# In the last batch's attention, ScalarE takes five of six drawn key blocks and the neighbours' V rows from VectorE; three of the first expert tiles' row gathers move to the end of the attention

## The chip, the cores and the metric

The kernel runs on one core of a Trainium2 chip. The metric is device time in microseconds (us). A profiled execution has, beside its time, a span: the time from its first to its last instruction. Engines are called as the profile calls them: PE is the matrix engine (TensorE), PEld its loading of stationary operands, DVE is VectorE, ACT is ScalarE, POOL is GpSimd, and SP is the engine that here only issues transfers.

## What is computed

Two stages, in 32-bit floats. First, block-sparse attention over 4 batches, 8 heads, 768 positions and head dimension 64, in blocks of 32. Then a mixture of experts over the resulting 3072 rows of 512 values: each row goes to its best of 8 experts.

```python
# attention: a query block sees its neighbours, the first and last block, and three drawn blocks
mask = np.abs(blk_i - blk_j) <= 1
mask = mask | (blk_i == 0) | (blk_j == 0) | (blk_i == n_blocks - 1) | (blk_j == n_blocks - 1)
for qb in range(n_blocks):
    for kb in sampled_blocks[qb]:
        mask[qb * 32:(qb + 1) * 32, kb * 32:(kb + 1) * 32] = True
attn = softmax(where(mask, q @ k.T / 8, -1e9)) @ v
x = attn.transpose(0, 2, 1, 3).reshape(3072, 512)
# experts
expert_idx = argmax(x @ w_gate); gate_w = softmax(x @ w_gate)[row, expert_idx]
out[row] = gate_w * (relu(x[row] @ w1[expert_idx]) @ w2[expert_idx])
```

## The kernel before

**Attention in steps.** A batch has 24 query blocks. They are worked off in six groups (numbered g; the order is 5, 0, 1, 2, 3, 4), a group of four blocks as two tiles of 64 queries; group 5 has one such tile, and the first and last block, which see every key. Each group takes two steps, one for each half of the heads, so there are 12 steps per batch and 48 in all, numbered i from 0. Batch 3, the last, has steps 36 to 47. Step i does the following, and each engine executes its share in program order, since the order of the attention is written out by hand:

- copies for step i + 2: `place_middle` (DVE, the neighbouring keys into `xk`, L539 and L540), `place_keys` (the six drawn key blocks of one query tile into `kr`, L555: three on ACT, then three on DVE; each block is a copy of 128 partitions by 4 x 32 values, and its column comes from a register that the engine loads from `from_k`, L550);
- the scores of step i on PE (`s`, L339 and L344), the exponentials on ACT (`ea`, L349), and the masks on DVE (L355), two each;
- the products with V of step i - 1 on PE (`attend`, L373), chunk by chunk: chunk 0 is neighbours' rows, chunks 1 and 2 hold gathered rows;
- every second step, PE turns a finished block of rows (`turn_out`, `xr`, L464), ACT copies it (`xo`, L466) and PE makes the gate's logits (L482);
- the division on DVE (`divide`: `sums` L442, `r` L444, `xb` L448), and in odd steps SP's transfer of `xb` to `x_rows` in DRAM (L454);
- in odd steps `place_values` for the next group but one step: neighbours' V rows into `around`, on ACT (L532) and DVE (L533).

**V's gathered rows.** `fetch_values(b, g, ti, ch)` (L515) makes POOL issue an indirect transfer of 128 rows, or 64, of 2080 bytes from `v_rows` into `around`. Four are issued per group, each behind `not_before` (L527), a one-element copy on POOL that makes the queue wait for something that DVE writes: `sums`, `xk`, `kr`'s last block, or a masked `ea`. The last of a group's four, (ti, ch) = (1, 1), is issued at the head of the group's first step and read by PE one step later.

**The routing, inside batch 3.** The first three batches' rows are finished by then. `early` does their sorting in steps 38 to 44, almost all on DVE: ranks, counts (`cnA`, L771), the expert numbers `xeA` (L792), slots, one-hots (L960), and the row lists `gA` (L995). From step 40 on, SP fetches the first two experts' weights in 16 parts of 512 KB (L1081, L1085), two per step. SP takes its work in order: parts stand behind the `xb` transfers of L454.

**The experts.** `gather(i)` (L1041) makes POOL gather the 128 rows of expert tile i from `x_rows` into `xg`, 2080 bytes each; `turn_x(i)` turns them on PE (L1110), with an ACT copy (L1111); `layer1` and `layer2` (L1121, L1135) follow. `turn_x(0)` stands after the scores of step 47, `turn_x(1)` inside `layer1(0)`, `turn_x(2)` inside `layer1(1)`. The gathers 0, 1 and 2 are issued at the ends of steps 44, 45 and 46; gather 3 at the start of the expert loop.

Of the kernel before, what the change touches and what calls it, by code (L numbers as in the profile page):

```python
# [17 lines left out]
def kernel(  # L18
# [11 lines left out]
    nc = tc.nc  # L30
    P = 128
    B, H, S, D = q.shape
    BLK = 32
    NB = S // BLK
    NR = sampled_blocks.shape[1]
# [76 lines left out]
    def held(flat):  # L112
        a, c = NPR * S, 2 * NPR * S
        return (
            flat[:, :a].rearrange("p (r s) -> p r s", r=NPR), flat[:, a:c].rearrange("p (r s) -> p r s", r=NPR),
            flat[:, c : c + NCH * VR].rearrange("p (c w) -> p c w", c=NCH),
        )

    sets = [held(other[:]), held(room[:])]
    sets = [sets[(b + B - 1) % 2] for b in range(B)]  # L120
# [5 lines left out]
    around = mpool.tile([P, 2, 5, VR], F32, name="around")  # L126
# [167 lines left out]
    def tiles_of(g):  # L294
        return (2 * g, 2 * g + 1) if g < GL else (2 * g,)

    def parity(b, g):
        return (b * NG + order.index(g)) % 2
# [19 lines left out]
    def plan_all(b, pr):  # L318
        kT = sets[b][0][:, pr, :]
        return [(j, at_cols(kT, c * P + j * D, D), all_queries(b, pr), c * D, D) for c in range(NCH) for j in range(2)], []  # L320
# [117 lines left out]
    def divide(b, g, half):  # L438
        bank, _ = banks_of.pop((b, g, half))
        op = bank[:, : 4 * (D + 4)].rearrange("p (a w) -> p a w", a=4)  # L440
        mine = sums[:, b * NG + g, 4 * half : 4 * half + 4]
        nc.vector.tensor_scalar_add(mine, op[:, :, D], 1e-9)  # L442
        r = small.tile([P, 4], F32, name="r", bufs=2)
        nc.vector.reciprocal(r[:], mine)  # L444
        if half == 0:
            xbs[(b, g)] = work.tile([P, DM], F32, name="xb")
        xb = xbs[(b, g)]
        nc.vector.tensor_tensor(  # L448
            xb[:, half * 4 * D : (half + 1) * 4 * D].rearrange("p (a d) -> p a d", a=4), op[:, :, :D],
            r[:].unsqueeze(2).to_broadcast([P, 4, D]), op=ALU.mult,  # L450
        )
        if half == 1:
            for p, n, row in pieces(g):
                nc.sync.dma_start(x_d[b * S + row : b * S + row + n, :DM], xb[p : p + n, :])  # L454

    def pieces(g):
        if g < GL:
            return [(0, P, BLK + P * g)]
        return [(0, D, BLK + P * g), (D, BLK, 0), (D + BLK, BLK, S - BLK)]
# [65 lines left out]
    def not_before(at):  # L525

        nc.gpsimd.tensor_copy(paced[:], at)  # L527

    def place_values(b, g):

        par, n = parity(b, g), len(tiles_of(g))
        nc.scalar.copy(around[:D, par, 1 : 1 + n, :], sets[b][2][:D, g : g + n, :])  # L532
        nc.vector.tensor_copy(around[D:, par, 0, :], sets[b][2][D:, g, :])  # L533

    def place_middle(b, g):
        to, kT = xk[:, parity(b, g)], sets[b][0]
# [5 lines left out]
    def place_keys(b, g, ti, prs=slice(0, NPR), on_vector=NR):  # L542

        t = tiles_of(g)[ti]
        par = parity(b, g)
        cut = 2 * NR - on_vector
        for nm, a, z in (("Activation", 0, cut), ("DVE", cut, 2 * NR)):
            if a == z:
                continue
            _, at = nc.values_load_multi_w_load_instructions(  # L550
                from_k[0:1, NR + 2 * NR * t + a : NR + 2 * NR * t + z], engines=(getattr(mybir.EngineType, nm),),
                min_val=0, max_val=S - BLK, skip_runtime_bounds_check_because="clamped on the chip to the blocks that there are",
            )
            for i, v_ in zip(range(a, z), at):
                (nc.scalar.copy if nm == "Activation" else nc.vector.tensor_copy)(  # L555
                    kr[:, par, ti, prs, i * BLK : (i + 1) * BLK], sets[b][0][:, prs, bass.ds(v_, BLK)],
                )
# [478 lines left out]
    def of(name, i, p):  # L1036
        return rt[name + "A"][:p, i : i + 1] if i < KA else rt[name + "B"][:p, i - KA : i - KA + 1]

    def gather(i):
        xg = st[i]["xg"] = keep_xg[i % 4]  # L1040
        nc.gpsimd.indirect_dma_start(  # L1041
            out=xg[:], out_offset=None, in_=x_d[: N - S, :] if i < KA else x_d[:, :], in_offset=bass.IndirectOffsetOnAxis(ap=of("g", i, P), axis=0),
        )
# [250 lines left out]
    def fill_next(b, n):  # L1294
        fill_stage(b, n // 2, n % 2, n // 2 % 2)

    steps = [(b, g, half) for b in range(B) for g in order for half in range(2)]
    for i, (b, g, half) in enumerate(steps):
        here = i % (2 * NG)
        prs = (2 * half, 2 * half + 1)  # L1300
        nxt = steps[i + 2] if i + 2 < len(steps) else None

        if nxt is not None:
            b_, g_, half_ = nxt
            if half_ == 0:
                place_middle(b_, g_)
        if half == 0 and i > 0 and len(tiles_of(g)) > 1:
            if nxt is not None:
                not_before(xk[0:1, parity(*nxt[:2]), 0, D : D + 1])
            fetch_values(b, g, 1, 1)  # L1310
        if nxt is not None and half_ < len(tiles_of(g_)):
            place_keys(b_, g_, half_)
        two = half == 1 and i + 1 < len(steps) and len(tiles_of(steps[i + 1][1])) > 1
        if two:
            b_, g_, _ = steps[i + 1]
            not_before(kr[0:1, parity(b_, g_), 1, 0, NKR - 1 : NKR])
            fetch_values(b_, g_, 1, 0)

        if g == GL:
            plans = [plan_all(b, pr) for pr in prs if b > 0] + [plan_two(b, prs)]  # L1320
            *e_alls, e = scores(*plans)
            masked_two(e)
            mine = [(b, g, pr, e_alls[pr % 2] if b > 0 else None, e) for pr in prs]
        else:
            found = scores(*[plan(b, g, pr) for pr in prs])
            for e in found:
                masked(e, g)
            mine = [(b, g, pr, None, e) for pr, e in zip(prs, found)]
        if b == B - 1:
            early(here)  # L1330
        if half == 1 and i + 1 < len(steps):
            not_before(mine[1][4][0:1, 0, 0:1])
            fetch_values(*steps[i + 1][:2], 0, 1)

        copy_turned = None
        if b + 1 < B:
            if b == 0 and here < 2:
                fill_next(1, 2 * here)
                fill_next(1, 2 * here + 1)
            if 2 <= here < 10:  # L1340
                copy_turned = turn(b + 1, (here - 2) // 2, here % 2, None, (here - 2) // 2 % 2)
                if here < 6:
                    fill_next(b + 1, here + 2)
        if b + 2 < B and here >= 8:
            fill_next(b + 2, here - 8)

        out_of = steps[i - 3][:2] if i >= 3 and half == 1 else None
        if copy_turned:
            copy_turned()
        if i > 0 and before[0][1] != GL:  # L1350
            attend(before, (lambda: turn_out(*out_of)) if out_of else None)
        elif i > 0:
            for n, (b_, g_, pr, e_all, e) in enumerate(before):
                attend_last(b_, pr, e_all, e)
                if n == 0 and out_of:
                    turn_out(*out_of)
        if "gates" in rt:
            gate_weights()
        if out_of:
            logits(*out_of)  # L1360
            if out_of[1] == order[-1]:
                gate(out_of[0])
        if i > 0:
            divide(*steps[i - 1])
        if half == 0 and nxt is not None:
            if i >= 2:
                fetch_ends(*nxt[:2])
                b_, g_, half_ = steps[i - 1]
                not_before(sums[0:1, b_ * NG + g_, 4 * half_ : 4 * half_ + 1])
            fetch_values(*nxt[:2], 0, 0)  # L1370
        if half == 1 and nxt is not None:
            place_values(*nxt[:2])
        if b + 1 < B:
            load_v(b + 1, V_AT[b > 0].get(here, ()))
            if 7 <= here < 10:
                keep_v(b + 1, (2 * here - 14, 2 * here - 13))
        if 3 <= i < 11:
            route_consts(i - 3)
        if i == 11:
            route_tokens()  # L1380
        if b == B - 1 and 8 <= here < 11:
            gather(here - 8)
        before = mine
    turn_x(0)
    attend(before)
    divide(*steps[-1])
    attn_by_hand.close()
    lend(lent, ps_h=2, ps_m=2, ps_z=2)
    layer1(0, lambda: turn_out_late(*steps[-1][:2]), lambda: turn_x(1))
# [5 lines left out]
    for i in range(NS):  # L1395
# [4 lines left out]
        here = AT_S.index(i) if i in AT_S else None  # L1400
# [160 lines left out]
```

## Time and profile before

| what | us |
|---|---|
| median of 3 runs | 654.19 |
| the three runs | 651.63, 654.19, 657.99 |
| the profiled execution, time | 664.23 |
| the profiled execution, span | 662.5 |
| batch 3's stage of expert weights, 246.2 to 299.6 | 53.4 |
| experts after it, 299.6 to the end | 362.9 |

The profiled execution is 10.0 us above the median of the three runs. Its busy times are PE 628.4 us (95% of the span), DVE 305.1 (46%), ACT 223.7 (34%), POOL 182.8 (28%). These are averages over stages with different limits: between 240 and 250 us DVE is busy for 9.04 us of 10, and after 299.6 us for a third of the time. The profile gives all positions in us from the span's start, and a line such as L533 is line 533 of the kernel before.

### The profile page before, as it was taken

The numbers are of one execution on the slowest core, as the hardware profiler recorded it, in microseconds if no ns is written. First come the engines' busy times: TensorE is split into PE (matmuls) and PEld (weight loads), VectorE is DVE, ScalarE is ACT, GpSimd is POOL, SyncE is SP. The second block draws the span as 40 slices with busy tenths as digits, with TensorE's granted clock in tenths as the row PEclk, the third lists the DMA queues.
The fourth block names the chain that finished last, engine by engine and source line by source line (L and its number), as shares of the span: only waits on it lengthen the run. The fifth ranks groups of instructions, "written<-read, shape, count | busy, mean of one in ns | idle before, by whom it ended". The sixth has DMA issues, their size and how long they took to land. (4 is left out here: it accounts for less than half of the span.)

```text
span 662.5 us, 21377 instructions
## 1 busy us (share of the span) xinstructions
PE 628.4 (95%) x8952; PEld 524.3 (79%) x8952; DVE 305.1 (46%) x978; ACT 223.7 (34%) x430; POOL 182.8 (28%) x288
## 2 busy tenths in 40 slices
PE   7999999999999998789999999999999999999995
PEld 7888889998999887679776677797769678767962
DVE  6456665774677498632750368200182023702200
ACT  5456756675676554422111011121111111111110
POOL 2146744552354244710111122001300203020210
PEclk7769999999999996969999999999999999999998
DMA  9579966996787237954788999959996699989950
GB/s 266 168 189 231 250 181 157 217 264 171 172 199 218 81 98 267 308 189 165 263 315 303 352 348 347 342 206 361 400 398 245 209 405 395 343 286 391 396 205 19
DMA packets 124857, 170.93 MB, mean 258 GB/s; under 512 B 71028, under 2 KB 71029, under 8 KB 124726
## 3 DMA queue, kind: packets, MB, share of 16 engines
q1 hardware_dynamic: 114688, 137.61, 63.4%
q0 software_dynamic: 10000, 31.59, 14.7%
q8 instruction: 80, 1.31, 0.8%
q14 instruction: 51, 0.42, 0.2%
q10 hardware_dynamic: 38, 0.00, 0.0%
HBM read 150.11 MB, written 19.33 MB: 256 GB/s over the span
## 5 line engine op out<-in xcount | busy, mean ns | idle before, releaser
L1121 PEld LDWEIGHTS hp<-around,room 128*128 128x128 f32 x1216 | 138.4, 192 | 8.3 <-issue 5.6
L1121 PE MATMUL hp<-around,room 128*128 128x128 f32 x1216 | 141.3, 276 | 2.0 <-ACT kr L1128 1.7
L1102 DVE STREAM_TRANSPOSE around<-xg 32x128 f32<-32x128 f32 x208 | 62.9, 302 | 126.1 <-PE hp L1121 95.9
L349 ACT ACTIVATE ea<-s 128x768 f32<-128x768 f32 x104 | 81.4, 811 | 104.7 <-PE s L344 70.8
L1135 PE MATMUL zp<-room,kr 128*128 128x512 f32 x256 | 112.7, 594 | 0.0
L515 POOL DMA_INDIRECT around<-v_rows,rows_of x88 | 95.1, 1081 | 62.4 <-issue 23.7
L373 PE MATMUL op<-around,ea 128*64 128x65 f32 x2112 | 92.0, 232 | 6.2 <-DMA around<-v_rows,rows_of 3.4
L373 PEld LDWEIGHTS op<-around,ea 128*64 128x64 f32 x2112 | 79.9, 143 | 14.9 <-issue 6.3
L1135 PEld LDWEIGHTS zp<-room,kr 128*128 128x128 f32 x256 | 47.5, 190 | 54.6 <-issue 54.6
L355 DVE TENSOR_TENSOR ea<-ea,mask 128x768 f32<-128x768 f32 x80 | 74.4, 957 | 20.6 <-ACT ea L349 14.7
L1128 ACT ACTIVATE kr<-hp 128x512 f32<-128x512 f32 x36 | 21.4, 598 | 119.1 <-PE hp L1121 104.9
L1150 POOL DMA_INDIRECT out_dram<-kr,sB x14 | 14.1, 1006 | 164.6 <-ACT kr L1140 106.1
L1140 ACT ACTIVATE kr<-zp,xg 128x512 f32<-128x512 f32 x16 | 11.0, 690 | 100.3 <-PE zp L1135 100.3
L1228 DVE STREAM_TRANSPOSE ea<-ea 32x128 f32<-32x128 f32 x84 | 21.7, 285 | 32.6 <-DMA ea<-x_rows,gB 31.9
L1150 POOL DMA_INDIRECT out_dram<-kr,sA x5 | 5.1, 1020 | 89.8 <-ACT kr L1140 89.8
L344 PE MATMUL s<-other,kr 64*128 64x64 f32 x352 | 29.4, 273 | 0.5 <-issue 0.2
L339 PE MATMUL s<-room 64*64 64x64 f32 x736 | 27.2, 249 | 2.2 <-issue 1.9
L344 PE MATMUL s<-room,kr 64*128 64x64 f32 x352 | 28.5, 267 | 0.7 <-issue 0.5
L344 PEld LDWEIGHTS s<-other,kr 64*128 64x128 f32 x352 | 27.4, 201 | 1.0 <-issue 0.9
L344 PEld LDWEIGHTS s<-room,kr 64*128 64x128 f32 x352 | 26.3, 194 | 1.3 <-issue 1.3
L339 PE MATMUL s<-other 64*64 64x64 f32 x736 | 25.0, 231 | 1.9 <-issue 1.4
L339 PEld LDWEIGHTS s<-room 64*64 64x64 f32 x736 | 22.0, 158 | 4.8 <-issue 3.4
(342 smaller groups left out, 870.7 us busy)
## 6 DMA issues: line engine op xcount, KB each, us to landing
room<-in_moe_w_dram SPq DMA_DIRECT2D x46, 2048.0 KB
room<-in_moe_w_dram SPq DMA_DIRECT2D x16, 512.0 KB
x_rows<-xb SPq DMA_DIRECT2D x20, 256.0 KB
room<-in_k_dram SPq DMA_DIRECT2D x24, 192.0 KB
room<-in_q_dram SPq DMA_DIRECT2D x24, 192.0 KB
v_rows<-room SPq DMA_DIRECT2D x12, 260.0 KB
v_rows<-other SPq DMA_DIRECT2D x12, 260.0 KB
room<-in_v_dram SPq DMA_DIRECT2D x16, 192.0 KB
```

Of the source, the lines that this page charges most:

```text
L339: nc.tensor.matmul(s[j * D : (j + 1) * D, hh, a : a + n], lhsT=keys(r), rhs=queries(r), start=True, stop=True)
L344: nc.tensor.matmul(s[:, hh, a : a + n], lhsT=keys(r), rhs=queries(r), start=True, stop=True)
L349: nc.scalar.activation(e, s[:, :, : 6 * D], AF.Exp, scale=scale)
L355: nc.vector.tensor_tensor(e, e, m[:, None, :].to_broadcast([P, 2, 6 * D]), op=ALU.mult)
L373: nc.tensor.matmul(op[ti * D : (ti + 1) * D, pr % 2, hh, : D + 1], lhsT=e, rhs=values[:, (2 * pr + hh) * VW : (2 * pr + hh + 1) * VW], sta ...
L515: nc.gpsimd.indirect_dma_start(out=around[p0:, par, 1 + ti + 2 * ch, :], out_offset=None, in_=v_d[b][:, :], in_offset=bass.IndirectOffsetO ...
L1102: nc.vector.transpose(xT[d, :, t], xg[t, :DM].rearrange("p (c q) -> p c q", c=DB)[:, :, d])
L1121: nc.tensor.matmul(hp[:, m, :], lhsT=st[i]["w1"][:, c, fb * P : (fb + 1) * P], rhs=st[i]["xT"][:, c, :], start=(c == 0), stop=(c == DB - 1),)
L1128: nc.scalar.activation(hT[:, g * (FB // 2) : (g + 1) * (FB // 2), :], hp[:], AF.Relu)
L1135: nc.tensor.matmul(zp[:], lhsT=st[i]["hT"][:, fb, :], rhs=st[i]["w2"][:, fb, :], start=(fb == 0), stop=(fb == FB - 1),)
L1150: ins = nc.gpsimd.indirect_dma_start(out=to[:, :], out_offset=bass.IndirectOffsetOnAxis(ap=at, axis=0), in_=rows, in_offset=None, bounds_c ...
L1228: nc.vector.transpose(xT_u[d, :, j * P + tq * 32 : j * P + (tq + 1) * 32], xg_u[t, j, :DM].rearrange("p (c q) -> p c q", c=DB)[:, :, d],)
```

## The change

For the last batch only (`b == B - 1`), `place_keys` is called with one block on VectorE in place of three, so ScalarE copies five of six; and `place_values` has its second copy on ScalarE too. The gathers of the first three expert tiles are issued later: gather 0 at the end of step 46 (it was 44); gather 1 at the end of step 47 behind a wait of POOL for step 47's masked `ea` (it was 45, without a wait); gather 2 after the last division (it was 46). Gather 3, which follows in the program, is thus also behind that wait. PE's order is the same in both kernels.

```diff
@@ place_values @@
         nc.scalar.copy(around[:D, par, 1 : 1 + n, :], sets[b][2][:D, g : g + n, :])
-        nc.vector.tensor_copy(around[D:, par, 0, :], sets[b][2][D:, g, :])
+        (nc.scalar.copy if b == B - 1 else nc.vector.tensor_copy)(around[D:, par, 0, :], sets[b][2][D:, g, :])
@@ the loop over steps @@
         if nxt is not None and half_ < len(tiles_of(g_)):
-            place_keys(b_, g_, half_)
+            place_keys(b_, g_, half_, on_vector=1 if b_ == B - 1 else NR)
...
-        if b == B - 1 and 8 <= here < 11:
-            gather(here - 8)
+        if i == len(steps) - 2:
+            gather(0)
+        if i == len(steps) - 1:
+            not_before(mine[1][4][0:1, 0, 0:1])
+            gather(1)
         before = mine
     turn_x(0)
     attend(before)
     divide(*steps[-1])
+    gather(2)
     attn_by_hand.close()
```

## The prediction

> **What bounds the kernel now.** I first read the page's rows of 40 slices (16.6 us each: busy tenths, PE's granted clock, DMA share):
>
> ```profile
> PE   7999999999999998789999999999999999999995
> DVE  6456665774677498632750368200182023702200
> PEclk7769999999999996969999999999999999999998
> DMA  9579966996787237954788999959996699989950
> ```
>
> PE is full nearly everywhere, but in slices 16 to 18 (249 to 299 us, batch 3 and its weight transfers) it and its clock sag. So I read windows of 10 us there (columns: busy us with counts for PE, PEld, DVE, ACT, POOL; clock; DMA share; GB/s):
>
> ```profile
> 240.00:250.00 10.00, 9.02 (x228) 7.90 (x228) 9.04 (x34) 5.75 (x12) 5.78 (x7) 1.00 0.58 154
> 250.00:260.00 10.00, 7.86 (x126) 7.30 (x128) 7.56 (x26) 3.81 (x8) 5.55 (x8) 0.61 0.93 324
> 260.00:270.00 10.00, 9.72 (x234) 9.08 (x230) 9.16 (x26) 5.74 (x12) 5.18 (x6) 0.87 0.62 211
> 270.00:280.00 10.00, 7.62 (x158) 6.26 (x156) 5.70 (x19) 2.61 (x7) 6.85 (x10) 0.98 0.97 322
> 280.00:290.00 10.00, 6.54 (x83) 5.74 (x84) 2.17 (x6) 2.46 (x4) 3.05 (x4) 0.50 0.77 267
> ```
>
> There are two holes, at 250 and at 276 to 286, with the clock at 0.5 after each. The timeline of PE names what ended each stop (in brackets: idle before, releaser):
>
> ```profile
> 251.07 0.44 PE L464 MATMUL xr<-ident,xb 128*128 128x128 f32 x2 [1.33 <-DVE xb L448]
> ...
> 253.30 0.92 PE L373 MATMUL op<-around,ea 128*64 128x65 f32 x12 [1.06 <-DMA around<-v_rows,rows_of]
> ...
> 277.38 0.39 PE L373 MATMUL op<-around,ea 128*64 128x65 f32 x5 [0.77 <-DMA around<-v_rows,rows_of]
> 278.10 0.29 PE L373 MATMUL op<-around,ea 128*64 128x65 f32 x2 [0.33 <-issue]
> ```
>
> **Hole 1** is DVE's lateness (1.33 us), then a V gather's (1.06), then about 10 us at half clock. Scores ended at 248.28 in step 41 and 258.94 in step 42: 10.66 us, where steps 44 and 45 took 4.9 to 5.0. The hole costs 5.7 us: 2.4 of waits, 3.3 of clock. **Hole 2** is another thing. From 276.2 to 285.6 PE issues one to six matmuls, pauses, and starts again every 0.72 us, mostly with "issue" as releaser: no engine and no buffer holds it. Scores ended at 274.07 in step 45 and 289.4 in step 46: 15.3 us, 10.3 too many. After 299.6 us PE is busy 350.5 of 355.4 us (to 655), at full clock; nothing of the change reaches there unless a row gather is late.
>
> [...] clock 0.50 follows both holes. [...] The page's queue q8 has 80 packets in 1.31 MB, so blocks of that size; hole 2 looks like one that came late, which no run here has shown yet. [...] in 248 to 250 us SP's queue moved 0.57 MB of weights and POOL's queue nothing, with a V gather issued at 247.53.
>
> **The change part by part.**
>
> *DVE loses.* Batch 3 has 11 query tiles and 6 groups: 22 copies of key blocks and 6 of V rows leave it. The timeline has three blocks from 246.65 and the next work at 247.06, so 0.14 each; L533 from 246.00 to 246.44, 0.44. In all 22 x 0.14 + 6 x 0.44 = 5.7 us. Only what lies ahead of a wait counts:
>
> ```profile
> 246.00 0.43 DVE L533 COPY around<-other 64x520 f32<-64x520 f32 x1
> 246.44 0.29 DVE L540 COPY xk<-other 128x256 f32<-128x256 f32 x1
> 246.65 0.49 DVE L555 COPY kr<-other 128x128 f32 x3
> ...
> 250.59 0.42 DVE L448 TENSOR_TENSOR xb<-op,r 128x256 f32<-128x256 f32 x1
> ```
>
> From 240.4 to this `xb` DVE has no gap: it is the bound. Taken out on that run: in step 38, 0.44 + 0.28, of which 0.42 count (the second mask waits for the exponential that ends at 234.71); 0.28 in step 39; 0.44 + 0.28 in step 40: 1.42 us. `xb` ends at 249.6 in place of 251.02. PE also loses its wait of 0.54 for `cnA` at 242.2 and wants `xb` at 249.2, so about 0.4 remains of the two waits: at the transposes PE is 1.4 us ahead.
>
> *What is late next.* PE then wants the (1, 1) gather at 250.8 (before: 252.24, had at 253.30). Its issue follows `xk`, 1.14 us earlier. But the first two weight parts went out at 246.25, before it, and they follow `xeA`, which moves only 0.42 + 0.28 = 0.7 us; the gather's bytes came after them. So it lands 0.7 to 1.14 earlier, and I take 0.7: PE restarts at 252.6. Of 1.4 us, 0.7 goes into a longer wait for V. PE still idles some 2 us together[...], so the 3.3 us stay.
>
> *The same in step 45.* DVE runs without a gap from 264.32 to 273.6; 0.28 + 0.44 is taken out ahead of `xk` (270.15 on POOL), so the gather of 270.87 goes 0.7 earlier, against a wait of 0.77: gain 0 to 0.7, taken 0.5, as weights crowd it too.
>
> *ACT gains.* Two more blocks per tile at 0.20 (three span 0.70, the first 0.30): 0.40; in odd steps also a 64x520 copy, 0.59 by L532 of that shape (216.66 to 217.25). In all 22 x 0.20 + 6 x 0.59 = 7.9 us on an engine that is busy 5.75 of 10. Ahead of an exponential it has 2.57 us of idle time where both come (step 40), 0.99 used. Tightest is step 41:
>
> ```profile
> 246.51 0.70 ACT L555 COPY kr<-other 128x128 f32 x3
> 247.79 1.51 ACT L349 ACTIVATE ea<-s 128x768 f32<-128x768 f32 x2 [0.58 <-PE s L344]
> ```
>
> 0.58 of slack against 0.40, and PE comes up to 0.5 sooner: the exponential may be 0.3 late, hidden since its products come a step later. Queued behind the new copies are only exponentials and `xo`; `kr` is wanted two steps on. Cost 0, at most 0.3 in each of 5 such steps.
>
> *Waits and register loads.* The V copies' wait for the old `around` to be read is the wait that L532 has already passed on ACT. POOL's wait on `kr` reads block 5, which stays with DVE. SP's order changes in one thing: three loads of expert numbers slide behind four weight parts, where SP anyway waits for `xb`. Cost 0.
>
> *The row gathers.*
>
> ```profile
> 275.08 1.27 POOL L1041 DMA_INDIRECT xg<-x_rows,gA  x1 [0.30 <-issue]
> 276.35 0.18 POOL L527 COPY paced<-kr 1x1 f32<-1x1 f32 x1
> ...
> 280.51 0.95 POOL L515 DMA_INDIRECT around<-v_rows,rows_of  x1 [0.30 <-issue]
> ```
>
> Gathers 0 and 1 leave V's way on POOL: 1.27 + 1.25 us, so V's last gather is issued near 278. Gathers 1 to 3 leave the crowded stretch up to 287 us: 3 x 128 x 2080 B = 0.8 MB, 2.0 us at the 390 GB/s seen there. In this profile PE wants that V only at 295, long after it lands; with hole 2 absent it would want it near 287, and it would land near 286 (issued by 281.5, plus the 4.4 us that the gather of 247.53 took from its issue's end at 248.9 to PE's start). Gain 0 to 1.0, taken 0. POOL now waits for step 47's mask (296.94) ahead of gathers 1, 2, 3 and nothing else: gather 1 is issued by 298.4, landed by 302.8 at 4.4, wanted by `turn_x(1)` at 303.71; the two others follow 1.25 us apart, wanted at 312.06 and 326.64. Gather 0, issued near 280, is wanted after 287. Cost 0; if gather 1 takes 2 us longer, 1.1.
>
> **Sum.** 0.7 + 0.5 = 1.2 us, between -1.5 (ACT) - 1.1 (gather 1) = -2.6 and 1.4 + 0.7 + 1.0 = 3.1, the clock apart. Against the profiled execution: 664.23 - 1.2 = 663.0, if hole 2 returns. That execution is 10.0 above the median of 654.19, and hole 2 costs 10.3: I choose to read the plain runs as mostly free of it. They hold hole 1, so 654.19 - 1.2 = **653.0**.
>
> **Rivals.**
> - *The clock stays full after hole 1.* [...] 3.3 us more come back; with the upper gains, up to 648. [...] 649.5; chance 0.20.
> - *A late instruction block* (slower). SP's bursts follow `xb`, now earlier, so 2 MB of weights (252.46) start 1.4 us sooner against a PE without its pause. A step uses a block in 5 us; DMA share is near 1 for 9 us at a time. [...] at the price of 10.3: 663. Against: steps 43 to 45 ran at 5 us between the bursts without it. Chance 0.18.
> - *ACT becomes the bound:* 0.3 x 5 with no gain: 655.5, chance 0.08.
> - *Nothing moves,* V's lateness taking all: 654.2, chance 0.07.
> - The forecast, 0.47.
>
> **The numbers.** A change under 1% (6.5 us) is about what a measurement of this kernel can't tell from none. Below 647.7 lies the rival of the clock with all upper gains, and a run set without any hole: 0.17. Above 660.7, the late block: 0.16. The rest is within: 0.67. The range runs from 646.5 (hole 1 gone, upper gains) to 661.5 (the crawl in part of the runs).
>
> **What will show it.** DVE busy near 8 of 10 in 240 to 250; the wait for `xb` at L464 under 0.5, the wait of L373 for `around` after it longer than 1.06; the clock at 0.5 after it; ACT's idle time ahead of L349 still above zero; gathers 1 to 3 after the last mask, with no wait at L1110. I am wrong if the wait for V is gone, if L349 waits for ACT's own copies, or if PE's "issue" pauses appear elsewhere or in the plain runs.

## The result and the profile after

| what | before | after |
|---|---|---|
| median, us (20 runs each) | 656.15 (650.19 to 663.95) | 652.86 (647.51 to 657.28) |
| the profiled execution, time | 664.23 | 649.58 |
| its span | 662.5 | 647.8 |
| batch 3 and its weights: first exponential of step 38 to the first matmul of `layer1` | 66.4 | 55.9 |
| from there to the end | 362.9 | 363.9 |

The ratio is **0.9951, with an interval of 0.9929 to 0.9973**: 3.3 us less by the medians. Ratios, here and below, leave out runs that are over 1.5% above the fastest of the same kernel. The two profiled executions lie 14.65 us apart, and most of that is chance: the one of before had the crawl of hole 2. The experts took 1 us more after. In the other profiles of this study, except that of no_weights below, they took between 362.9 and 365.6, so no gain or cost shows there.

The page's 40 slices of the changed kernel (16.2 us each):

```profile
PE   7979899999999998999999999999989999999995
DVE  6557565765677386635810494202190024602200
PEclk8779999999999996999999999999999999999998
DMA  8579976897787347967889999779994799989950
```

Apart from the start and the end, only slice 15 (243 to 259 us) still has a lower clock. The windows of the same kernel over the stage (columns as in the prediction), then three of 1 us:

```profile
240.00:250.00 10.00, 7.23 (x161) 6.32 (x157) 8.01 (x25) 5.74 (x15) 6.70 (x8) 0.81 0.86 282
250.00:260.00 10.00, 10.00 (x176) 9.38 (x174) 6.82 (x19) 4.81 (x11) 3.37 (x6) 0.68 0.68 224
260.00:270.00 10.00, 9.28 (x247) 8.39 (x242) 8.28 (x22) 8.24 (x20) 7.38 (x9) 1.00 0.95 321
270.00:280.00 10.00, 9.24 (x244) 8.51 (x246) 5.16 (x11) 4.23 (x6) 3.13 (x5) 1.00 0.99 330
...
243.00:244.00 1.00, 0.18 (x2) 0.00 (x0) 0.90 (x4) 0.15 (x1) 0.18 (x1) 1.00 0.95 356
244.00:245.00 1.00, 0.97 (x20) 0.81 (x20) 0.97 (x2) 0.44 (x1) 0.84 (x1) 1.00 0.90 349
245.00:246.00 1.00, 0.19 (x6) 0.05 (x1) 1.00 (x3) 1.00 (x2) 0.99 (x2) 1.00 0.78 298
```

DVE has 8.01 us of ten in the first window, where before had 9.04. But the two windows hold different steps, since step 38 begins 5.24 us earlier after the change. The same stretch of work, shifted by these 5.24 us:

```profile
234.76:244.76 10.00, 9.16 (x242) 8.23 (x242) 9.32 (x33) 7.48 (x18) 6.90 (x9) 1.00 0.62 199
```

There DVE is busy for 9.32 us, and its timeline shows no gap from 228.80 to the end of step 41's `xb` at 243.97. So DVE still bounds this `xb`; it only reaches it sooner. PE worked 1.34 us of the three ahead of 246, and the clock then ran at half until 256: 0.81 and 0.68 are 2 x (0.19 + 0.32) x 10 = 10.2 us at half clock, as before. From 260 on it is full. The timeline of PE says why the first stop stayed:

```profile
244.03 0.44 PE L464 MATMUL xr<-ident,xb 128*128 128x128 f32 x2 [0.84 <-DVE xb L448]
247.12 1.02 PE L373 MATMUL op<-around,ea 128*64 128x65 f32 x13 [1.93 <-DMA around<-v_rows,rows_of]
...
269.56 0.67 PE L373 MATMUL op<-around,ea 128*64 128x65 f32 x7 [0.71 <-issue]
270.99 0.62 PE L373 MATMUL op<-around,ea 128*64 128x65 f32 x13 [0.76 <-DMA around<-v_rows,rows_of]
...
281.42 0.41 PE L482 MATMUL xr<-wg,xo 128*64 128x8 f32 x9 [1.05 <-issue]
```

The wait for `xb` is 0.84 us in place of 1.33, the wait for V after it 1.93 in place of 1.06: together 2.77, where before had 2.39. Of hole 2 waits of 0.71 and 0.76 us are left, and a pause of 1.05 us comes later, at 281.42. ACT's timeline up to the exponentials of steps 40 and 41:

```profile
236.57 0.62 ACT L533 COPY around<-other 64x520 f32<-64x520 f32 x1
237.20 1.09 ACT L555 COPY kr<-other 128x128 f32 x5
238.20 1.50 ACT L349 ACTIVATE ea<-s 128x768 f32<-128x768 f32 x2
239.87 1.10 ACT L555 COPY kr<-other 128x128 f32 x5 [0.17 <-issue]
241.63 1.51 ACT L349 ACTIVATE ea<-s 128x768 f32<-128x768 f32 x2 [0.67 <-PE s L344]
```

The moved copies are there. The exponential at 241.63 waits for PE, the one at 238.20 stands right behind ACT's own copies. And POOL's timeline for the row gathers:

```profile
272.95 0.95 POOL L1041 DMA_INDIRECT xg<-x_rows,gA  x1 [0.30 <-issue]
280.14 0.18 POOL L527 COPY paced<-ea 1x1 f32<-1x1 f32 x1 [6.24 <-DVE ea L355]
280.80 0.97 POOL L1041 DMA_INDIRECT xg<-x_rows,gA  x1 [0.48 <-issue]
```

Gather 1 waits 6.24 us for the mask of step 47; `turn_x(1)` at 288.01 shows no wait.

### The profile page after: what moved, and what is told of

Read it like the earlier page. It is cut to its first block, busy times and chain, and to the rows that moved or that the text cites. A ratio compares the mean times of both kernels' runs of the same rounds, so it can differ in the third digit from the quotient of the medians.

```text
span 647.8 us, 21381 instructions
## 1 busy us (share of the span) xinstructions
PE 612.7 (95%) x8952; PEld 512.9 (79%) x8952; DVE 298.1 (46%) x950; ACT 231.7 (36%) x458; POOL 186.6 (29%) x289
## 3 DMA queue, kind: packets, MB, share of 16 engines
q8 instruction: 80, 1.31, 0.8%
## 5 line engine op out<-in xcount | busy, mean ns | idle before, releaser
L349 ACT ACTIVATE ea<-s 128x768 f32<-128x768 f32 x104 | 79.7, 809 | 79.5 <-PE s L344 69.9
L373 PE MATMUL op<-around,ea 128*64 128x65 f32 x2112 | 89.8, 229 | 12.5 <-DMA around<-v_rows,rows_of 8.5
L373 PEld LDWEIGHTS op<-around,ea 128*64 128x64 f32 x2112 | 77.8, 141 | 21.3 <-DMA around<-v_rows,rows_of 9.7
L344 PE MATMUL s<-other,kr 64*128 64x64 f32 x352 | 26.7, 266 | 0.2 <-issue 0.2
L344 PE MATMUL s<-room,kr 64*128 64x64 f32 x352 | 26.1, 260 | 0.0
L339 PE MATMUL s<-room 64*64 64x64 f32 x736 | 25.0, 249 | 0.5 <-DVE room L158 0.3
L344 PEld LDWEIGHTS s<-other,kr 64*128 64x128 f32 x352 | 24.8, 194 | 0.3 <-issue 0.3
L344 PEld LDWEIGHTS s<-room,kr 64*128 64x128 f32 x352 | 24.2, 188 | 0.0
L344 PE MATMUL s<-room,xk 64*128 64x128 f32 (+1 forms) x192 | 23.1, 308 | 1.1 <-issue 1.1
L344 PE MATMUL s<-other,xk 64*128 64x128 f32 (+1 forms) x192 | 22.7, 313 | 0.0
```

What stands on the lines that cost most here:

```text
L339: nc.tensor.matmul(s[j * D : (j + 1) * D, hh, a : a + n], lhsT=keys(r), rhs=queries(r), start=True, stop=True)
L344: nc.tensor.matmul(s[:, hh, a : a + n], lhsT=keys(r), rhs=queries(r), start=True, stop=True)
L349: nc.scalar.activation(e, s[:, :, : 6 * D], AF.Exp, scale=scale)
L373: nc.tensor.matmul(op[ti * D : (ti + 1) * D, pr % 2, hh, : D + 1], lhsT=e, rhs=values[:, (2 * pr + hh) * VW : (2 * pr + hh + 1) * VW], sta ...
```

## The experiments

The theory: DVE's lead is the gain, and V's gather, behind SP's weight parts, takes half of it back. The rivals: the moved row gathers are the gain; the plain runs only seem to differ; the pauses of PE are late instruction blocks that the change shifts (a block is a packet of the page's queue q8, of the kind instruction: 80 packets of 16 KB each). All ratios are to the kernel before on the same chip. "Half clock" is the mean over all runs of 2 x (1 - granted clock) x span. In the change's profile the same 48 products with V took 1.62 us at full clock and 2.87 at half, so an estimated 0.44 us is lost in each us at half clock. In every profile 25 to 33 us of it lie before 50 us and at the very end, outside the stage of interest.

| kernel | ratio (95% interval) | median, us | runs | half clock, us |
|---|---|---|---|---|
| the change | 0.9951 (0.9929, 0.9973) | 652.86 | 20 | 41.3 |
| copies_only | 0.9953 (0.9929, 0.9977) | 652.90 | 22 | 41.6 |
| gathers_only | 0.9983 (0.9959, 1.0007) | 655.22 | 22 | 44.0 |
| keys_only | 0.9981 (0.9955, 1.0007) | 656.19 | 22 | 44.5 |
| vrows_only (second chip) | 0.9986 (0.9962, 1.0010) | 666.05 | 22 | 51.1 |
| weights_later | 0.9886 (0.9835, 0.9937) | 649.15 | 6 | 36.5 |
| before_later | 1.0019 (0.9995, 1.0043) | 657.94 | 22 | 45.9 |
| weights_half | 0.9798 (0.9747, 0.9849) | 644.38 | 6 | 30.7 |
| weights_half_2 (third chip) | 0.9893 (0.9844, 0.9943) | 647.04 | 6 | 35.7 |
| before_half (second chip) | 0.9964 (0.9939, 0.9990) | 666.35 | 22 | 51.8 |
| before_half_2 (third chip) | 0.9940 (0.9913, 0.9966) | 653.99 | 22 | 42.6 |

The kernel before had medians of 656.6 to 657.0 (half clock 45.2 to 45.5) on the first chip, 667.3 (50.7) on the second, 655.8 (45.5) on the third.

**The parts of the change.** copies_only is the change with the row gathers left at the ends of steps 44 to 46; gathers_only is the reverse, shown here as its edit to the changed kernel:

```diff
-        (nc.scalar.copy if b == B - 1 else nc.vector.tensor_copy)(around[D:, par, 0, :], sets[b][2][D:, g, :])
+        nc.vector.tensor_copy(around[D:, par, 0, :], sets[b][2][D:, g, :])
...
-            place_keys(b_, g_, half_, on_vector=1 if b_ == B - 1 else NR)
+            place_keys(b_, g_, half_)
```

> Only the copies move to ScalarE; the row gathers stay at the ends of steps 44 to 46. Theory 1 (the gain is VectorE's: about 1 us of earlier steps 39 to 41, the rest of its lead lost in a longer wait for V): 0.998 to 0.995 of the kernel before, most or all of the change's 0.9951. Theory 2 (the gain is the gathers': 0.8 MB and two POOL slots out of the crowded stretch): 0.999 to 1.000. In the profile both expect the wait for xb at L464 near 0.8 us and the wait for V after it near 1.9, with the clock at 0.5 behind them.

> Only the row gathers move; VectorE keeps its copies. Theory 1: 1.000 to 0.998. Theory 2: 0.997 to 0.995, and the last V gathers issued some 2.5 us earlier than before. In the profile both expect hole 1 as in the kernel before: 1.3 us for xb, 1.1 us for V, then half clock.

The copies alone bring what the whole change brings (0.9953 against 0.9951). Two sets of runs with the copies are clear of 1, so the plain runs do not only seem to differ. The gathers alone cannot be told from nothing. That they are the whole gain is ruled out: 0.9951 lies outside their interval.

Then the copies split in two, on the kernel before: only `on_vector=1 if b_ == B - 1 else NR` (keys_only), or only the line of `place_values` (vrows_only).

> The kernel before with only the key blocks on ScalarE (five of six), V's rows left to VectorE. By the times taken out on the run up to step 41's xb: 0.28 in each of three steps of 1.42 us, so the wait for xb falls from 1.3 by about 0.4 (net of PE's own 0.5 gained at cnA), and the gain is half or more of that of all copies (0.9953): 0.998 to 0.9965.

> The kernel before with only the second copy of V's rows on ScalarE. By the times taken out ahead of step 41's xb it is 0.44 twice of 1.42 us in all, of which 0.14 to 0.44 of the first counts; the key blocks alone gave 0.9981. If the parts simply add up to the copies' 0.9953: 0.9965 to 0.998. If the wait for xb has to fall under the point at which the clock halves, neither part does it alone: 0.998 to 1.000.

Neither half alone is clear of 1. Their product, 0.9967, lies inside the interval of copies_only, though they ran on different chips; which of the two copies counts more is not settled. The wait for `xb` did not fall with the key blocks alone, as had been expected, nor with the V rows alone:

```profile
253.90 0.44 PE L464 MATMUL xr<-ident,xb 128*128 128x128 f32 x2 [1.32 <-DVE xb L448]
249.68 0.44 PE L464 MATMUL xr<-ident,xb 128*128 128x128 f32 x2 [1.32 <-DVE xb L448]
```

The first line is of keys_only, the second of vrows_only; half clock follows in both. Only with both copies moved is the wait 0.83 to 0.85 us.

**What takes the lead back.** The parts of the weights are issued one step later, on the change (weights_later) and on the kernel before (before_later), the last two after the attention:

```diff
-        for n in range(2 * (i - 4), 2 * (i - 3)):
+        for n in range(2 * (i - 5), 2 * (i - 4)):
...
+    early(12)
```

> The changed kernel, with the 16 parts of the first experts' weights each fetched one step later, the last two after the attention. Theory A (hole 1's wait for V is the weights' doing: the first two parts stand ahead of the gather of step 40 in the DMA engines): the wait of 1.9 us at L373 in step 41 is gone, the one for xb of 0.8 stays, and the clock stays full behind it, so steps 41 to 43 take 5 us each and the time falls by 1.9 + 3 us against the changed kernel, 0.988 to 0.991 of the kernel before. Theory B (the gather is late by its own latency of 4 us, whatever else moves): the wait stays near 1.9, the clock halves, and the time is the changed kernel's, 0.995. If the next bunch of parts only catches the gather of step 42, the hole moves by two steps and the time is between them.

> The kernel before with its weight parts one step later and nothing else, the last two after the attention. If V's wait behind the first parts and VectorE's lateness are separate losses, the weights alone bring what they brought on top of the change, 0.9886 / 0.9951 = 0.9935. If the change's lead on VectorE can only be used when V is not late, the two together bring more than the product: then this is 0.996 or above.

PE's timeline in weights_later:

```profile
243.75 0.44 PE L464 MATMUL xr<-ident,xb 128*128 128x128 f32 x2 [0.85 <-DVE xb L448]
...
255.81 0.62 PE L373 MATMUL op<-around,ea 128*64 128x65 f32 x13 [1.07 <-DMA around<-v_rows,rows_of]
266.30 0.49 PE L373 MATMUL op<-around,ea 128*64 128x65 f32 x7 [1.38 <-issue]
```

In step 41 the wait for `xb` is the same 0.85 us, the wait for V is gone, and the clock stays full there: from the exponential of step 41 to that of step 42 took 6.1 us (9.96 in the change). So it was the weights ahead of V that kept hole 1 open. In before_later V is not late either, yet PE's timeline has the old wait:

```profile
252.79 0.44 PE L464 MATMUL xr<-ident,xb 128*128 128x128 f32 x2 [1.31 <-DVE xb L448]
```

That wait alone was enough for 6.8 us at half clock from 254.8. A second spell of 6.8 us came at step 45, behind a pause of 1.97 us by "issue", and there was no gain in time (1.0019). Later weights need the lead that the change gives. All weights after the attention (`range(0, 16 * (i == 12))`, no_weights, one execution) shows the other end:

> The changed kernel with none of the experts' weights fetched during the attention; all 16 parts follow it. Late-block theory: with the DMA engines uncrowded, the instruction blocks of PE come every 230 to 290 PE instructions instead of once after 440, PE has no pause with the releaser issue over 0.5 us and no wait for V in steps 41 to 47, and steps 42 to 47 take 5 us each: from the first exponential of step 38 to the first matmul of layer1 about 51 us against 55.9 in the changed kernel's profile. Rival (the pauses come from the semaphores or the register loads of PE's own queue): they stay. The experts then wait for their weights, so the whole is slower, by 5 us or more.

```profile
246.39 0.44 PE L464 MATMUL xr<-ident,xb 128*128 128x128 f32 x2 [0.85 <-DVE xb L448]
256.17 0.44 PE L464 MATMUL xr<-ident,xb 128*128 128x128 f32 x2 [0.87 <-DVE xb L448]
285.28 0.77 PE L1121 MATMUL hp<-around,room 128*128 128x128 f32 x2 [7.25 <-DMA room<-in_moe_w_dram]
```

Of waits over 0.5 us, PE's timeline has only the two for `xb` up to the experts: no wait for V, no pause by "issue". But the experts then wait 7.25 us for their first weights: the stage takes 55.0 us, where 51 was expected, and the time is 656.65. Between the ends lies one part per step, with eight parts after the attention:

```diff
-        for n in range(2 * (i - 4), 2 * (i - 3)):
+        for n in range(i - 4, 16 if i == 12 else i - 3):
...
+    early(12)
```

> The changed kernel with one weight part per step (8 in steps 40 to 47: the first layer's weights of both experts), the 8 of the second layer after the attention. Theory A (V's gathers and PE's instruction blocks queue behind bunches of 2 MB): bunches of 1 MB end before either is wanted, hole 1 keeps only the wait of 0.8 for xb, the clock stays full, and the stage takes 51 to 52 us; the later weights cost the experts 0 to 1.5: 0.986 to 0.990 of the kernel before, at or below the 0.9886 of the weights one step later. Theory B (any weights ahead of the gather of step 40 suffice): hole 1 as before, 0.994 to 0.996.

> The changed kernel with one part per step (eight after the attention), a second time and beside its counterpart on the same chip. Both theories: ratio to before 0.976 to 0.985 as the first time (0.9798), half clock per run 28 to 35 us, no pause of PE over 1 us in steps 41 and 45. Against it: were its first result a matter of few runs, the ratio would be 0.985 to 0.995. By theory A it should be the product of 0.995 (the change) and before_half_2's ratio; by theory B it is clearly lower than that product.

This has **the lowest ratio here, 0.9798, and on another chip 0.9893**, below the change's 0.9951 in both. The first lies below the 0.986 to 0.990 that was expected. The second lies above the 0.976 to 0.985 that was expected of a repeat, in the range that was named for a first result owed to few runs, and it is not clear of weights_later's 0.9886. The windows of weights_half_2:

```profile
240.00:250.00 10.00, 8.96 (x234) 7.98 (x230) 9.48 (x29) 7.46 (x18) 7.49 (x9) 1.00 0.76 242
250.00:260.00 10.00, 9.61 (x266) 8.75 (x260) 9.44 (x25) 7.90 (x21) 7.18 (x9) 1.00 0.71 219
260.00:270.00 10.00, 10.00 (x278) 9.27 (x274) 7.57 (x22) 5.67 (x10) 8.24 (x10) 1.00 0.83 268
```

The DMA share is 0.71 to 0.83, where the change had up to 0.95, and the clock is 1.00 in all three. Both ratios are clear of 1; how large the gain is, stays less sure: six runs each.

Is it a gain by itself? The same edit on the kernel before:

> The kernel before with one weight part per step and the second layer's 8 after the attention, nothing else. Theory A ([...] VectorE's lateness of 1.3 us is enough to halve the clock by itself, as in the profile of the kernel before with later weights, where the window was 61% busy): the wait of 1.3 for xb stays with half clock behind it, step 45 has no pause, and the ratio is 0.985 to 0.991; the change is then worth 0.6 to 1% on uncrowded DMA engines, more than the 0.5% that it brought. Theory B (crowding is all): 0.979 to 0.983, as with the change.

> The kernel before with one part of the first experts' weights per step (eight of them after the attention), a second time, since the first time its profile held a crawl of PE with pauses each 0.72 us, as before's own first profile did. Theory A (the weights' bunches and DVE's lateness are two separate debts; the crawl hid half of it): a clear gain of its own, ratio 0.985 to 0.992, half clock per run falling from about 45 us to under 40. Theory B (without DVE's lead the wait for xb of 1.3 us halves the clock whether V is late or not, so the weights' spacing is worth little without the copies): ratio 0.995 to 1.000 as the first time (0.9964), half clock per run within 3 us of before's.

The first ran on the second chip, where its profile and that of vrows_only both crawled as before's first had; its 0.9964 lies outside both ranges. The profile of the second is free of the crawl. Its 0.9940 fell between what the two theories there allowed, but it rests on 14 of the 22 runs, against all 27 of the kernel before. Over all runs the medians, 653.99 and 655.77, stand at 0.997, and half clock, 42.6 against 45.5, fell by no more than theory B said. So a gain of the spacing by itself is not shown. With 0.9940 the product with the change, 0.9951 x 0.9940 = 0.9891, is weights_half_2's 0.9893; but weights_half (0.9798) lies below its product (0.9915), and weights_later (0.9886) below its own (0.9970). Whether the two edits multiply stays open. The profile of before_half_2 shows one more thing, first in PE's timeline and then in POOL's:

```profile
280.46 0.68 PE L373 MATMUL op<-around,ea 128*64 128x65 f32 x14 [1.08 <-DMA around<-v_rows,rows_of]
282.24 0.33 PE L373 MATMUL op<-around,ea 128*64 128x65 f32 x2 [1.09 <-DMA around<-v_rows,rows_of]
284.36 1.02 PE L373 MATMUL op<-around,ea 128*64 128x65 f32 x13 [1.79 <-DMA around<-v_rows,rows_of]
```

```profile
275.71 1.41 POOL L1041 DMA_INDIRECT xg<-x_rows,gA  x1 [0.30 <-issue]
277.42 0.95 POOL L515 DMA_INDIRECT around<-v_rows,rows_of  x1 [0.30 <-PE s L344]
278.68 1.29 POOL L1041 DMA_INDIRECT xg<-x_rows,gA  x1 [0.30 <-issue]
```

PE, which comes this early, waits 4 us for V, and row gathers stand ahead of and behind the last V gather. weights_half_2, which has the gathers moved, waits for V only once, 0.19 us; it differs in the copies too. In one profile each this points to a worth of the move that appears only when the rest is faster; it was not measured alone there.

**The pauses by "issue".** First a second execution of the kernel before, unchanged:

> The kernel before, unchanged, for a second profile of it. If the crawl of 9 us at 276 to 286 (hole 2) belongs to the kernel, it is there again; if it is an accident of one execution, the profile has hole 1 with half clock behind it but no row of pauses with the releaser issue every 0.72 us, and a time near the median of 656.

```profile
273.52 0.34 PE L373 MATMUL op<-around,ea 128*64 128x65 f32 x4 [1.15 <-issue]
274.68 0.33 PE L373 MATMUL op<-around,ea 128*64 128x65 f32 x2 [0.82 <-DMA around<-v_rows,rows_of]
275.66 0.76 PE L373 MATMUL op<-around,ea 128*64 128x65 f32 x13 [0.65 <-DMA around<-v_rows,rows_of]
```

Its timeline of PE has no crawl: one pause, two waits, and a time of 655.65. So the crawl is not in every execution of this kernel. The pauses can be placed by counting: windows that begin at 0 give how many matmuls and weight loads PE had done. The change up to its two pauses, copies_only up to one of its own, and before up to the first pause of its crawl:

```profile
0.00:269.50 269.50, 250.07 (x6341) 232.11 (x6342) 175.34 (x506) 172.31 (x350) 127.78 (x228) 0.94 0.77 205
0.00:281.40 281.40, 260.11 (x6597) 241.20 (x6598) 180.51 (x517) 177.03 (x356) 132.18 (x234) 0.95 0.78 210
```

```profile
0.00:278.90 278.90, 256.42 (x6469) 237.91 (x6470) 177.81 (x512) 174.96 (x353) 132.70 (x234) 0.94 0.77 205
```

```profile
0.00:276.10 276.10, 259.77 (x6342) 238.85 (x6342) 181.41 (x533) 163.77 (x321) 124.34 (x227) 0.94 0.75 200
```

At 269.5 and at 276.1 us, in two kernels, PE stops within one instruction of the same place. From 6341 and 6342 to 6597 and 6598 are 512 instructions, to 6469 and 6470 are 256. The blocks come about as often: between 204 and 250 us of the kernel before they start 221 to 287 PE instructions apart, 254 and 4.96 us on the mean. That these pauses sit on block borders, 256 instructions apart, is an estimate from these counts. Counted so, eight of the fourteen profiles stop for 0.51 to 1.97 us at this first place. The starts of the 16 KB packets agree: in the change one came 442 instructions after the one ahead (at 267.06 us, in the crowd of weights), while in no_weights, which has no such pause, they came every 210 to 294. The times agree too. In all twelve pauses over 0.5 us at such borders, eight profiles together, PE starts again 1.24 to 1.74 us after the end of the last packet; in no_weights, weights_half, weights_half_2 and before_half_2, which do not stop at the first place, the packet had ended 2.0 to 3.2 us before PE came there. So the pauses of 0.5 to 2.0 us go with late blocks; that PE stands for want of the instructions in them is inferred from these times. The crawl only begins at such a border; its stops come every 0.72 us, a few matmuls apart, and before's went on to 285.3 us though a packet had ended at 279.45; in before_half they came though packets had started at 275.8 and 280.0. What makes it stays open, and whether the change crawls on the second chip was not tried.

## Why the prediction was right, and where its sum was short

The sign was right; the predicted gain was 1.2 us, the measured one 3.3. That the time fits so closely (653.0 against 652.86) is luck: the median of three runs that it starts from, 654.19, lies 1.96 us below the median of 20, 656.15, and this made up for the gain that was 2.1 us too small. From 656.15 the same sum gives 654.95. By its steps, with times counted from the first exponential of step 38 (233.20 before, 227.96 after):

- **DVE loses 5.7 us:** it lost 7.0 (305.1 to 298.1 us). `xb` of step 41 ended 1.80 us earlier, not 1.42. DVE near 8 of 10 in 240 to 250 came, but only because the window had moved to other steps; at the same steps it is 9.32.
- **PE is there 0.54 us sooner:** it was 1.31 sooner. 0.91 of it was gained by the end of step 41's scores, and 0.40 in the products after them, where PE before waited 0.19 us for a mask of DVE, which the sum left out. So the wait for `xb` fell to 1.33 - 1.80 + 1.31 = 0.84, not 0.4; PE's transposes gained 1.80, not 1.4.
- **The V gather lands 0.7 us earlier:** 0.94. The expert numbers released the weights 0.98 us earlier, and the gather behind them took 4.43 us from its issue's end to PE's start (before 4.44). This step decided what was left of the lead, and weights_later shows its cause. The longer V wait and the half clock after it came as written: hole 1 took 9.96 us from exponential to exponential, 10.0 before.
- **Step 45, taken as 0.5, and "the clock apart": this is the term that was mis-sized.** The best pair of profiles is b_again and the change, both without the crawl. From the first exponential of step 38 to `layer1` they take 59.4 and 55.9 us, 3.4 apart. Of this, 0.8 is gained up to step 42, as the sum had it (0.7); 0.3 is lost from there to step 45; 2.8 is gained between the exponentials of steps 45 and 46 (9.78 and 6.98 us); the last 0.1 comes after. There b_again waits 1.15, 0.82 and 0.65 us and then runs 6.8 us at half clock; the change waits 0.71 and 0.76, and the clock stays full. So the rival that lets the clock stay full named the right effect, but looked for it after hole 1.
- **How far this carries:** before (both), keys_only and before_later have a second spell of half clock at step 45; the change and copies_only have none. But gathers_only, whose ratio is 0.9983, has none either, and weights_later has one after its pause of 1.38 us. One profile each, so the place is likely and not shown. Over the runs, half clock fell from 45.2 to 45.5 us per run (the kernel before in the later comparisons) to 41.3, by 4.1 with a 95% interval of 1.6 to 6.6. By the 2.87 against 1.62 us above, that is an estimated 1.8 us of time, with the rest of the 3.3 left to shorter waits.
- **ACT gains 7.9 us at no cost:** 8.0 (223.7 to 231.7). Three exponentials (227.96, 238.20, 262.61) stand right behind ACT's copies, so "above zero" failed there, and with it a named sign of being wrong came; but nothing on PE waited for ACT there.
- **The row gathers, 0:** alone 0.9983 with 1 inside the interval; with the copies nothing more. The cover named (V wanted later) held in the change and was gone in before_half_2.
- **Hole 2:** reading the plain runs as mostly free of it was right as far as one execution tells: b_again has a time of 655.65 without the crawl. But it has pauses at the same place, which the sum did not count, and the change has two by "issue", another named sign of being wrong. That hole 2 is a late block was half right: the pauses go with late blocks, the crawl is not shown to. The slower rival, in which earlier bursts bring the crawl on, did not come true.

## What to carry to other kernels

When an engine that is late is relieved, ask which transfer is next and what its queue has just put ahead of it: here a lead of 1.8 us met a gather behind 1 MB of prefetch, and half of it was lost. Prefetch that is early enough can be spread out; half of it per step and the rest later, with the relief, was worth two to four times the relief alone. And where half clock follows a wait (6.8 us of it behind the 1.31 us in before_later), count it in the wait's cost, and look at waits together: in b_again three waits of 0.65 to 1.15 us within 3.41 us were followed by half clock, while one of 1.07 in weights_later was not. Last, compare windows that hold the same work: the same numbers on the clock of the profile held other steps after the change.

## What was not expected of the hardware

- The clock went to half behind windows in which PE was busy. The traces of before and after have every change of the clock whole multiples of 3.41 us from the next: in this stage half clock from 252.28 to 262.52 and from 279.58 to 293.24 us before, from 246.24 to 256.48 after. In the windows of 3.41 us just ahead of these three PE was busy 58, 44 and 45%. In all profiles, no_weights' idle one apart, such windows after which the clock was 0.5 had PE busy 29 to 61% in this stage, and those of 68% and more kept it full. A wait of 1.31 us was followed by half clock (before_later), one of 0.85 was not (weights_later). The busy share is no rule, though. Elsewhere in the profiles windows of 53% (weights_half_2, from 64.4 us) and 62% (gathers_only, from 97.2) kept it full, and windows of 69% (b_again, from 159.9) and 73% (weights_half, from 162.6) were followed by half clock. What decides stays open.
- Twelve waits of PE whose releaser is "issue", 0.5 to 2.0 us each, ended 1.24 to 1.74 us behind the end of an instruction block. At the first place counted, the window of 10 us around the pause had a DMA share of 0.95 to 1.02; with no weights in the attention (0.38 to 0.43 from 240 to 270) there was no pause.
- One chip ran the kernel before in 667.3 us, two others in 655.8 to 657.0. The difference, 10.3 to 11.5 us, is about the price of the crawl (10.3), and both profiles from that chip have it. That the chip brings the crawl on is not shown.
